# Two chained MLP layers behind a linear-attention stage: block 0's up projections as 256-token half-products

## The chip, the core and the metric

One core of one Trainium2 chip runs the whole program. The metric is device time in microseconds (us), lower is better. The engines are named as the profile names them: PE is TensorE's matrix multiply, PEld its weight load, DVE is VectorE, ACT is ScalarE, and SP only issues DMAs. All engines run side by side and wait for one another through semaphores; each works through its own instructions in the order in which the program gives them.

## What is computed

```python
gamma = 1.0 - 2.0 ** (-5.0 - np.arange(H))            # B, H, S, D = 2, 8, 768, 64
for t in range(S):
    state = gamma * state + einsum('bhd,bhe->bhde', k[:, :, t], v[:, :, t])
    y[:, :, t] = scale * einsum('bhd,bhde->bhe', q[:, :, t], state)
x = y.transpose(0, 2, 1, 3).reshape(1536, 512)
h = x @ w_in                # 512 -> 2048
x = (h * clip(h + 3, 0, 6) / 6) @ w_out               # layer 0
h = x @ moe2_w_in
out = (h * tanh(log1p(exp(h)))) @ moe2_w_out          # layer 1 (Mish)
```

Matrices are float32. The kernel computes each product of float32 matrices from halves: a high half (the value rounded to the matmul's format, `fp32r`) and a low half (what the rounding left), as high·high + low·high + high·low, so three matmuls stand for one.

## The kernel before, in words

**Tiles.** The 1536 tokens are three blocks of 512 (block 0, 1, 2). For each layer the 2048 hidden features are 16 tiles of 128 (index f), two tiles make a pair p, and two pairs make one of four groups g. An up projection of a tile and a block is 4 slices of the 512 inputs x 3 matmuls = 12 matmuls with 128 rows, 128 weight columns and 512 moving columns. It lands in one PSUM bank (`wk`, four of them), ACT and DVE turn it into g (layer 0: ACT `t` = relu(h + 3), DVE g = min(t, 6)·h; layer 1: ACT Mish). Then ACT writes the high half `gh`, DVE the low half `gl`, and a down projection of 12 matmuls adds the tile to four PSUM banks `acc`. There are 96 of these downs (2 layers x 4 groups x 3 blocks x 4 tiles), and so 96 instructions that write `gl`.

**Pairs of blocks.** Group 0 of layer 0 is *plain*: each block has its own 12-matmul up projections. In the seven other groups, blocks 1 and 2 and the two tiles of a pair are a 2 x 2 block product made with seven products in place of eight (`up_pair`, Winograd's form): products 1, 5, 2, 6, 3, 7, 4 of 6 matmuls each go into three banks X, Y, Z, ACT copies partial sums out (`snap`), DVE adds them (`plus`). Product 6 adds to X once product 1 has been copied, 7 adds to X once 6 has been copied, 4 adds to X once the sum of 7 has been taken. They need sums of weight quarters (`wsh`, `wsl`) and differences of x quarters (`make_forms`: T1 to T4, float32 in buffers `q`). Block 0 stays plain in all eight groups.

**Weights.** They come in as 64-bit words (`raw`) and are converted to float32 with integer operations: per chunk of 512 columns one `abs` (ACT in layer 0, DVE in layer 1) and four DVE operations (L405 to L410 of the listing), then the high half on ACT and the low half on DVE (`halves`). A pair has four chunks: two for up, two for down.

**Order.** `Plan` is a list scheduler that runs when the program is built. Each task has an engine, an assumed duration, buffers and dependencies; `order` fills the engines in order of start time and rank. The ranks of PE's work come from a loop that walks `downs` and `ups` with a clock: a down goes as soon as its source is older than `LEAD`, else the next up product goes; `GATE` holds back layer 1's ups. The attention stage's order is the string `EARLY`, that of its loads `LOADS`.

Of the kernel before, what the change touches and what calls it, by code (L numbers as in the profile page):

```python
# [35 lines left out]
BUFS = dict(wk=4, raw=2, cvu=1, cvd=2, t=1, gh=2, gl=2, E=2, R=2,  # L36
            qk=3, kv=3, A=2, kp=1, qs=1, st=3, qtab=2, rawA=1, wbh=3, wbl=3, wsh=3, wsl=3, wdh=4, wdl=4, q=5)

DMA512 = 1.28
MMR = 0.2266  # L40
DVE1 = 0.686
# [5 lines left out]
LEAD = (7.8, 7.5)  # L47
GATE = {'c': 5.0, 'w': 11.5}
EARLY = "sssbkbbkksskkbkbssbhskkbsbkkbohsbohhhhhsosbobohhohoohhoooo"
LOADS = "qk0 mask qk1 qk2 qk3 kv1 kv0 kv2 t1 kv3"  # L50
# [131 lines left out]
def body(ctx: ExitStack, tc: tile.TileContext, aps: dict, out: bass.AP):  # L182
# [37 lines left out]
    def wk():  # L220
        return buf("wk", [P, 512], "wk")
# [103 lines left out]
    def sq_up(u):  # L325
        seq(u, (12 if u[0] == "c" else 6) * MMR)
# [19 lines left out]
    while i < ND or hq < len(ups):  # L346
        nxt = ups[hq] if hq < len(ups) else None
        gate = 0.0
        if nxt and nxt[1] == 1:
            gate = max((done_at.get(b, 1e9) + GATE[nxt[0]]) for b in ((nxt[3],) if nxt[0] == "c" else (1, 2)))  # L350
# [23 lines left out]
    wbase, wsum, wdown = {}, {}, {}  # L374
    ld_w = [None]
    n_raw = [0]

    def words_of(layer, f, half, cb, col):

        nm = f"w{layer}_{f}_{half}"  # L380
        n_raw[0] += 1
        early = layer == 0 and f < 2 * NP and n_raw[0] % 3 == 0
        rb = buf("att", [P, 512], "rawA", I64) if early else buf("fix", [P, 512], "raw", I64)
        src = aps["w1" if layer == 0 else "w2"][f, half]
        ld = add(nm, "SP", DMA512, [], [rb], lambda: nc.sync.dma_start(out=rb.tile, in_=src))
        ld.after = ld_w[0]
        ld_w[0] = ld

        def words():
            w = rb.tile.bitcast(I32).rearrange("p (n t) -> p n t", t=2)  # L390
            return w[:, :, 0], w[:, :, 1]

        def c():
            return cb.tile[:, col:col + 512]

        def ci():
            return cb.tile.bitcast(I32)[:, col:col + 512]
        if layer == 0:
            a0 = add(nm + "abs", "ACT", act(512), [ld], [rb, cb],
                     lambda: A.activation(c(), words()[1].bitcast(F32), AF.Abs))  # L400
        else:
            a0 = add(nm + "abs", "DVE", dve(512, False), [ld], [rb, cb],
                     lambda: V.tensor_scalar(ci(), words()[1], 0x7FFFFFFF, None, ALU.bitwise_and))
        a1 = add(nm + "c", "DVE", dve(512, False), [a0], [cb],
                 lambda: V.tensor_scalar(c(), c(), TOP_MAX, TOP_MIN, ALU.min, ALU.max))  # L405
        a2 = add(nm + "t", "DVE", dve(512, False), [a1], [cb],
                 lambda: V.tensor_scalar(ci(), ci(), 3, 0x3FFFFFF8, ALU.logical_shift_left, ALU.bitwise_and))
        a3 = add(nm + "o1", "DVE", dve(512), [a2], [cb, rb], lambda: V.scalar_tensor_tensor(
            out=ci(), in0=words()[0], scalar=29, in1=ci(), op0=ALU.logical_shift_right, op1=ALU.bitwise_or))
        a4 = add(nm + "o2", "DVE", dve(512), [a3], [cb, rb], lambda: V.scalar_tensor_tensor(  # L410
            out=ci(), in0=words()[1], scalar=-0x40000000, in1=ci(), op0=ALU.bitwise_and, op1=ALU.bitwise_or))
        if early:
            att_tasks.append(a4)
        return a4

    def halves(nm, cb, c0, n, hb, lb, h0, deps):

        a = add(nm + "hi", "ACT", act(n), deps, [cb, hb],
                lambda: A.copy(hb.tile[:, h0:h0 + n], cb.tile[:, c0:c0 + n]))
        return a, add(nm + "lo", "DVE", dve(n), [a], [cb, hb, lb], lambda: V.tensor_tensor(  # L420
            out=lb.tile[:, h0:h0 + n], in0=cb.tile[:, c0:c0 + n], in1=f32(hb.tile)[:, h0:h0 + n],
# [4 lines left out]
    def make_pair(layer, p):  # L426
        nm = f"u{layer}_{p}"
        cb = buf("fix", [P, 1024], "cvu")
        bh, bl = buf("fix", [P, 1024], "wbh", F32R), buf("fix", [P, 1024], "wbl", F32R)
        sums = not plain[layer, p // NP]  # L430
        early = layer == 0 and p == 0

        def down(k):
            f = 2 * p + k
            db = buf("fix", [P, 512], "cvd")
# [437 lines left out]
```

## Time and profile before

| | us |
|---|---|
| median of 3 runs | 564.93 (564.76 to 565.51) |
| the profiled execution | 564.76 |
| its span, first to last instruction | 563.0 |
| PE busy | 549.9 (98%) |
| DVE busy | 416.1 (74%) |
| ACT busy | 275.5 (49%) |

The profiled execution's own time is 1.8 us more than its span. Busy time is the time in which at least one instruction of the engine was running. Matmul records overlap, since the end of one lies behind the start of the next, so the time that one matmul costs is read from start to start.

### The profile page before, as it was taken

The numbers are of one execution on the slowest core, as the hardware profiler recorded it, in microseconds if no ns is written. First come the engines' busy times: TensorE is split into PE (matmuls) and PEld (weight loads), VectorE is DVE, ScalarE is ACT, GpSimd is POOL, SyncE is SP. The second block draws the span as 40 slices with busy tenths as digits, with TensorE's granted clock in tenths as the row PEclk, the third lists the DMA queues.
The fourth block names the chain that finished last, engine by engine and source line by source line (L and its number), as shares of the span: only waits on it lengthen the run. The fifth ranks groups of instructions, "written<-read, shape, count | busy, mean of one in ns | idle before, by whom it ended". The sixth has DMA issues, their size and how long they took to land.

```text
span 563.0 us, 7604 instructions
## 1 busy us (share of the span) xinstructions
PE 549.9 (98%) x2932; PEld 455.9 (81%) x2932; DVE 416.1 (74%) x730; ACT 275.5 (49%) x506; POOL 0.2 (0%) x4
## 2 busy tenths in 40 slices
PE   6899999999999999999999999999999999999997
PEld 5798888887888888887888888888888888888875
DVE  2899998589959983689999999699426997821433
ACT  3899553665526533454537644534524442423330
POOL 0000000000000000000000000000000000000000
PEclk9999999999999999999999999999999999999999
DMA  8995323022312330013121124224200233000103
GB/s 334 399 358 205 113 76 119 33 75 76 101 49 75 115 111 1 1 38 113 37 76 34 42 75 116 72 79 150 72 0 2 77 111 112 1 0 2 75 17 133
DMA packets 15301, 51.66 MB, mean 92 GB/s; under 512 B 1697, under 2 KB 1697, under 8 KB 15265
## 3 DMA queue, kind: packets, MB, share of 16 engines
q1 hardware_dynamic: 15264, 51.17, 27.2%
q8 instruction: 23, 0.38, 0.3%
q14 instruction: 14, 0.11, 0.1%
HBM read 48.02 MB, written 3.15 MB: 91 GB/s over the span
## 4 chain that ended last, share of the span: by engine, by line
PE 90%; DMA 3%; DVE 3%; ACT 3%; SPq 0%; issue 0%; DVEq 0%; ACTq 0%
PE acc L214 49%; PE wk L214 41%; DMA qk<-in_qk_dram 2%; DMA kv<-in_kv_dram 2%; ACT kp L503 1%; DVE sb L768 0%; DVE g L685 0%; SPq L228 0%; DVE gs L622 0%; DVE wdl L420 0%; ACT st L524 0%; ACT q L569 0%; DVE gs L685 0%; ACT t L621 0%; DVE wsl L420 0%
## 5 line engine op out<-in xcount | busy, mean ns | idle before, releaser
L717 DVE TENSOR_TENSOR gl<-g,gh 128x512 fp32r<-128x512 f32 x68 | 46.8, 689 | 39.5 <-ACT gh L715 32.3
L214 PE MATMUL acc<-gh,wdh 128*128 128x512 f32 x192 | 75.0, 391 | 0.4 <-ACT gh L715 0.4
L214 PE MATMUL acc<-gl,wdh 128*128 128x512 f32 x192 | 74.8, 390 | 0.2 <-DVE gl L717 0.2
L214 PE MATMUL acc<-gh,wdl 128*128 128x512 f32 x192 | 74.7, 389 | 0.0
L214 PE MATMUL acc<-wdh,gh 128*128 128x512 f32 x192 | 74.7, 389 | 0.0
L214 PE MATMUL acc<-wdl,gh 128*128 128x512 f32 x192 | 74.7, 389 | 0.0
L214 PE MATMUL acc<-wdh,gl 128*128 128x512 f32 x192 | 74.7, 389 | 0.0
L715 ACT CAST gh<-g 128x512 fp32r<-128x512 f32 x68 | 42.3, 622 | 40.9 <-PE acc L214 28.6
L214 PE MATMUL wk<-xch,wbh 128*128 128x512 f32 x128 | 50.0, 391 | 0.0
L214 PE MATMUL wk<-xcl,wbh 128*128 128x512 f32 x128 | 49.8, 389 | 0.0
L214 PE MATMUL wk<-xch,wbl 128*128 128x512 f32 x128 | 49.8, 389 | 0.0
L214 PEld LDWEIGHTS acc<-gh,wdh 128*128 128x128 f32 x192 | 36.0, 188 | 8.7 <-ACT gh L715 0.8
L214 PEld LDWEIGHTS acc<-gl,wdh 128*128 128x128 f32 x192 | 36.0, 188 | 8.1 <-DVE gl L717 0.6
L214 PEld LDWEIGHTS acc<-wdh,gh 128*128 128x128 f32 x192 | 36.0, 188 | 7.5
L214 PEld LDWEIGHTS acc<-wdl,gh 128*128 128x128 f32 x192 | 36.0, 188 | 7.5
L214 PEld LDWEIGHTS acc<-wdh,gl 128*128 128x128 f32 x192 | 36.0, 188 | 7.5
L214 PEld LDWEIGHTS acc<-gh,wdl 128*128 128x128 f32 x192 | 36.0, 188 | 7.4
L715 ACT CAST gh<-gs 128x512 fp32r<-128x512 f32 x28 | 17.5, 624 | 33.8 <-PE acc L214 33.6
L685 DVE TENSOR_TENSOR g<-wk,g 128x512 f32<-128x512 f32 x22 | 15.2, 690 | 24.6 <-PE wk L214 23.2
L717 DVE TENSOR_TENSOR gl<-gs,gh 128x512 fp32r<-128x512 f32 x28 | 19.3, 688 | 18.5 <-ACT gh L715 13.6
L214 PE MATMUL wk<-q,wsh 128*128 128x512 f32 x84 | 32.7, 389 | 0.0
L621 ACT ACTIVATE t<-wk,bias 128x512 f32<-128x512 f32 x30 | 20.6, 688 | 21.9 <-PE wk L214 17.8
(116 smaller groups left out, 1110.0 us busy)
## 6 DMA issues: line engine op xcount, KB each, us to landing
raw<-in_w_dram SPq DMA_DIRECT2D x62, 512.0 KB, 3.5
kv<-in_kv_dram SPq DMA_DIRECT2D x12, 516.0 KB, 7.0
qk<-in_qk_dram SPq DMA_DIRECT2D x12, 512.0 KB, 6.9
out_dram<-sb SPq DMA_DIRECT2D x12, 256.0 KB, 2.1
qtab<-in_tabs_dram SPq DMA_DIRECT2D x5, 256.0 KB, 7.2
rawA<-in_w_dram SPq DMA_DIRECT2D x2, 512.0 KB, 7.4
mask<-in_mask_dram SPq DMA_DIRECT2D x1, 512.0 KB, 4.3
```

What stands on the lines that cost most here:

```text
L214: nc.tensor.matmul(o, l, r, start=start, stop=stop, skip_group_check=True)
L503: A.activation(kpb.tile[:, hs], kb.tile[:, hs], AF.Copy, scale=kb.tile[:, 2 * DM + h:2 * DM + h + 1])
L621: lambda: A.activation(tb.tile, src.tile, AF.Relu, bias=bias3))
L685: return add(f"c{k}_{nm}", "DVE", DVE1, deps, [ps, gb], lambda: V.tensor_tensor(out=gb.tile, in0=ps.tile, in1=gb.tile, op=ALU.add))
L715: a = add(f"hi{i}", "ACT", act(512), [tg, prev_split[0]], [gb, gh], lambda: A.copy(gh.tile, gb.tile))
L717: lambda: V.tensor_tensor(out=gl.tile, in0=gb.tile, in1=f32(gh.tile), op=ALU.subtract))
```

## The change

- **Block 0 as a pair.** In the seven groups that are not plain, block 0's tokens are cut into halves of 256, and the halves and the two tiles of a pair go through the same seven products (`up_pair` with `who` = "v"), each of 6 matmuls with 256 moving columns. Both halves share a bank: X and Y use columns 0 to 255, Z columns 256 to 511. Per pair two plain up projections (24 matmuls of 512 columns) become 42 matmuls of 256 columns.
- **New work for that.** Per pair three ACT copies and three DVE sums of 256 columns; g of the second tile in two halves; block 0's x in float32 (buffers `qc`) and its four differences with their halves, once per layer.
- **PSUM.** `wk` (four banks) becomes two rings of two, `wx` for X and `wy` for Z and Y; plain products and scores alternate between them.
- **Weights.** 1024 columns are converted at a time (the first pair of layer 0 still 512). A quarter of the up weights that only the plain product reads is now kept for plain pairs alone, in `tv`, so that `wbh` and `wbl` shrink to 768 columns.
- **Order.** Product 4 stands behind the first product of the next pair; `EARLY`, `LOADS`, `LEAD`, `GATE` have new values.

```diff
+GG, GS = 4, 4
-            qk=3, kv=3, A=2, kp=1, qs=1, st=3, qtab=2, rawA=1, wbh=3, wbl=3, wsh=3, wsl=3, wdh=4, wdl=4, q=5)
+            qk=3, kv=3, A=2, kp=1, qs=1, st=3, qtab=2, wbh=3, wbl=3, wsh=3, wsl=3, wdh=4, wdl=4, q=5, qc=5, tv=2)
-LEAD = (7.8, 7.5)
-GATE = {'c': 5.0, 'w': 11.5}
+LEAD = (7.2, 6.1)
+GATE = {'c': 8.0, 'w': 8.5, 'v': 8.0}
...
-            if k == "p":
+            if k == "p" or kind != "plain":
                 for p in range(g * NP, (g + 1) * NP):
-                    ups.extend(("w", layer, p, n) for n in (1, 5, 2, 6, 3, 7, 4))
+                    ups.extend(("w" if k == "p" else "v", layer, p, n) for n in (1, 5, 2, 6, 3, 7, 4))
...
+    for n in range(len(ups) - 2, -1, -1):
+        if ups[n][0] != "c" and ups[n][3] == 4 and ups[n + 1][0] == ups[n][0] and ups[n + 1][1] == ups[n][1]:
+            ups[n], ups[n + 1] = ups[n + 1], ups[n]
...
+    def words_of(layer, p, half, cb, parts):
+        rb = buf("fix", [P, 1024], "raw", I64)
...
+            n = 1024 // parts
...
+            a1 = add(nm + "c", "DVE", dve(n, False), [a0], [cb],
...
-    def make_forms(layer, after):
+    def make_forms(layer, who):
...
+            ba, bb, n = 0, 0, TB // 2
+            ta, tb = slice(0, TB // 2), slice(TB // 2, TB)
...
-    def up_pair(layer, p):
-        X, Y, Z = wk(), wk(), wk()
+    def up_pair(who, layer, p):
+        X, Z, Y = wk("x"), wk("y"), wk("y")
+        nm = f"{who}{layer}_{p}"
+        forms = tform[layer, who]
+        if who == "w":
+            pass_us, first, last = MMR, slice(0, TB), slice(0, TB)
...
+            pass_us, first, last = MMH, slice(0, TB // 2), slice(TB // 2, TB)
+            g11, g21 = [gbuf(layer, 2 * p + k, 0) for k in range(2)]
+            g12, g22 = g11, g21
...
+            gval[layer, f, 0] = (g11, [mish_or_swish(f"{layer}_{f}_0", layer, g11, [c11, c12])])
+            gval[layer, f + 1, 0] = (g22, [mish_or_swish(f"{layer}_{f + 1}_0d", layer, g22, [c22], last),
+                                           mish_or_swish(f"{layer}_{f + 1}_0c", layer, g22, [p4], first, X)])
```

On PE, at the turn from the second to the third group of layer 0, block 0's up projections of the third group stand before as four plain products (`wk`; `xch`, `xcl` are block 0's halves, `wbh`, `wbl` those of the weights), with a down behind:

```order
L214 MATMUL wk_1797<-xch_169,wbh_1343 128x512
L214 MATMUL wk_1797<-xch_169,wbl_1354 128x512
L214 MATMUL wk_1797<-xcl_192,wbh_1343 128x512
...
L214 MATMUL wk_1823<-xch_169,wbh_1343 128x512
...
L214 MATMUL wk_1849<-xch_169,wbh_1493 128x512
...
L214 MATMUL wk_1875<-xch_169,wbh_1493 128x512
...
L214 MATMUL acc_486_1756<-gh_1845,wdh_1414 128x512
```

At the same turn after, products of three pairs follow each other (the first matmul of each; `wx_1551`, `wx_1612`, `wx_1815` are the pairs' X, `tv` and `qc` hold differences of block 0's x): 4 of the first pair, then 5, 6, 2, 3 and 7 of the second around it, 1 of the third, 4 of the second.

```order
L216 MATMUL wx_1551<-tv_1209,wbh_1014 128x256
...
L216 MATMUL wy_1767<-xch_162,wsh_1376 128x256
...
L216 MATMUL wx_1612<-tv_1286,wsh_1376 128x256
...
L216 MATMUL wy_1789<-xch_162,wbh_1317 128x256
...
L216 MATMUL wx_1612<-xcl_183,wsh_1376 128x256
...
L216 MATMUL wx_1815<-xch_162,wbh_1480 128x256
...
L216 MATMUL wx_1612<-tv_1209,wbh_1317 128x256
```

Between product 7 of the second pair and its product 4 there is one product of another pair; the plain products waited for no copy.

On DVE, at the turn from layer 0 to layer 1, the work before (`cvd` a weight chunk, `gs` a pair's sum, `xcl` block 0's new x, `gl` a down's low half):

```order
L405 TENSOR_SCALAR cvd_3003<-cvd_3003 128x512
L458 TENSOR_TENSOR cvu_2747<-cvu_2747 128x256
L407 TENSOR_SCALAR cvd_3003<-cvd_3003 128x512
L784 TENSOR_TENSOR xcl_3021<-sb_382_1046,xch_2971 128x512
L408 SCALAR_TENSOR_TENSOR cvd_3003<-raw_2780,cvd_3003 128x512
L685 TENSOR_TENSOR gs_659_2930<-wk_2884,gs_659_2930 128x512
L420 TENSOR_TENSOR wsl_3036<-cvu_2747,wsh_3019 128x1024
L410 SCALAR_TENSOR_TENSOR cvd_3003<-raw_2780,cvd_3003 128x512
```

and after, with the chunk at 1024 columns, block 0's x in halves, and its differences behind (`qc`):

```order
L419 TENSOR_SCALAR cvd_3106<-cvd_3106 128x1024
L781 TENSOR_TENSOR gl_3122<-g_638_3104,gh_3112 128x512
L421 TENSOR_SCALAR cvd_3106<-cvd_3106 128x1024
L855 TENSOR_TENSOR xcl_3098<-qc_3068,xch_3033 128x256
L422 SCALAR_TENSOR_TENSOR cvd_3106<-raw_2775,cvd_3106 128x1024
L855 TENSOR_TENSOR xcl_3098<-qc_3070,xch_3033 128x256
L424 SCALAR_TENSOR_TENSOR cvd_3106<-raw_2775,cvd_3106 128x1024
...
L623 TENSOR_TENSOR qc_3027<-qc_3035,qc_3027 128x512
...
L623 TENSOR_TENSOR qc_3035<-qc_3070,qc_3035 128x512
```

Fewer and longer conversions, with a down's low half and block 0's x in the gaps between them, and new differences of x in the same stretch.

## Rows read from the trace of the kernel before

**Rows 1.** The page: busy time and share of PE and DVE, granted clock in 40 slices.
```profile
PE 549.9 (98%) x2932; PEld 455.9 (81%) x2932; DVE 416.1 (74%) x730; ACT 275.5 (49%) x506; POOL 0.2 (0%) x4
...
PEclk9999999999999999999999999999999999999999
```

**Rows 2.** The page: chain that ended last, by engine.
```profile
PE 90%; DMA 3%; DVE 3%; ACT 3%; SPq 0%; issue 0%; DVEq 0%; ACTq 0%
```

**Rows 3.** Busy time by stretch (us from the span's start; columns named in the first line).
```profile
core 0: us, PE busy (x) PEld busy (x) DVE busy (x) ACT busy (x) POOL busy (x), PEclk, DMA share, GB/s
0.00:32.00 32.00, 25.28 (x376) 22.05 (x376) 18.91 (x34) 20.96 (x66) 0.20 (x4) 1.00 0.95 366
...
245.00:353.00 108.00, 107.10 (x473) 88.31 (x472) 103.14 (x184) 56.63 (x90) 0.00 (x0) 1.00 0.24 71
353.00:388.00 35.00, 35.00 (x156) 28.96 (x156) 27.84 (x53) 16.47 (x27) 0.00 (x0) 1.00 0.29 89
...
540.00:563.00 23.00, 18.40 (x80) 14.56 (x79) 9.87 (x15) 5.50 (x9) 0.00 (x0) 0.97 0.25 92
```

**Rows 4.** Waits of PE: total us, times, longest.
```profile
PE wk L214 <- DMA qk<-in_qk_dram: 2.6, 2, 1.5
...
PE wk L214 <- ACT gs L682: 0.9, 1, 0.9
PE wk L214 <- DVE g L685: 0.9, 1, 0.9
```

**Rows 5.** Matmuls of block 0's plain products, one of three such rows.
```profile
L214 PE MATMUL wk<-xch,wbh 128*128 128x512 f32 x128 | 50.0, 391 | 0.0
```

**Rows 6.** Timeline (start us, length us): a run of 512-column matmuls and one load.
```profile
149.64 0.39 PE L214 MATMUL wk<-xch,wbl 128*128 128x512 f32 x1
...
150.10 0.39 PE L214 MATMUL wk<-xch,wbh 128*128 128x512 f32 x1
150.10 0.19 PEld L214 LDWEIGHTS wk<-xch,wbl 128*128 128x128 f32 x1
...
155.99 0.39 PE L214 MATMUL acc<-gl,wdh 128*128 128x512 f32 x1
```

**Rows 7.** Timeline: the first loads and matmuls after a wait of PE.
```profile
259.95 0.19 PEld L214 LDWEIGHTS wk<-xbl,wsh 128*128 128x128 f32 x1 [1.32 <-ACT gs L682]
259.96 0.50 PE L214 MATMUL wk<-xbl,wsh 128*128 128x512 f32 x1 [0.90 <-ACT gs L682]
260.06 0.19 PEld L214 LDWEIGHTS wk<-xbl,wsl 128*128 128x128 f32 x1
260.30 0.40 PE L214 MATMUL wk<-xbl,wsl 128*128 128x512 f32 x1
```

**Rows 8.** Timeline of DVE where it runs without a gap.
```profile
313.53 0.68 DVE L768 SCALAR_TENSOR_TENSOR sb<-acc,sb 128x512 f32<-128x512 f32 x1
314.13 0.42 DVE L458 TENSOR_TENSOR cvu<-cvu 128x256 f32<-128x256 f32 x1
314.46 0.68 DVE L420 TENSOR_TENSOR wdl<-cvd,wdh 128x512 fp32r<-128x512 f32 x1
...
315.40 0.42 DVE L403 TENSOR_SCALAR cvd<-raw 128x512 int32<-128x512 int32 x1
315.73 0.42 DVE L458 TENSOR_TENSOR cvu<-cvu 128x256 f32<-128x256 f32 x1
...
318.88 1.22 DVE L420 TENSOR_TENSOR wsl<-cvu,wsh 128x1024 fp32r<-128x1024 f32 x1
320.01 0.68 DVE L410 SCALAR_TENSOR_TENSOR cvd<-raw,cvd 128x512 int32<-128x512 int32 x1
```

**Rows 9.** Timeline of DVE: the 36th and the 64th of the 96 `gl`.
```profile
244.67 0.69 DVE L717 TENSOR_TENSOR gl<-gs,gh 128x512 fp32r<-128x512 f32 x1
...
388.35 0.69 DVE L717 TENSOR_TENSOR gl<-g,gh 128x512 fp32r<-128x512 f32 x1
```

**Rows 10.** Groups by shape: ACT copies of 256 and of 512 columns out of PSUM.
```profile
L569 ACT COPY q<-acc 128x256 f32<-128x256 f32 x16 | 5.4, 381 | 1.5 <-DVE xal L563 1.5
...
L682 ACT COPY g<-wk 128x512 f32<-128x512 f32 x22 | 12.9, 587 | 18.3 <-PE wk L214 18.3
```

More of the change, by code (lines that the diff above doesn't have):

```diff
@@ L372, in body @@
     t_warm = add("warm", "PE", 1.8, [z0], [zb] + kv_acc, run_warm, -99)
-    wbase, wsum, wdown = {}, {}, {}
+    wbase, wquart, wsum, wdown = {}, {}, {}, {}
     ld_w = [None]
[L376 to L414, printed above, removed]
@@ L427, in make_pair @@
         nm = f"u{layer}_{p}"
[L428 to L431, printed above, removed]
-        def down(k):
-            f = 2 * p + k
-            db = buf("fix", [P, 512], "cvd")
-            dh, dl = buf("fix", [P, 512], "wdh", F32R), buf("fix", [P, 512], "wdl", F32R)
-            t = words_of(layer, f, 1, db, 0)
-            hi, lo = halves(f"d{layer}_{f}", db, 0, 512, dh, dl, 0, [t, gate_hi[0]])
-            gate_hi[0] = hi
-            wdown[layer, f] = (dh, dl, lo)
@@ L441, in make_pair @@
-        base = []
-        for k in range(2):
-            t = words_of(layer, 2 * p + k, 0, cb, 512 * k)
-            hi, lo = halves(nm + f"b{k}", cb, 512 * k, 512, bh, bl, 512 * k, [t, gate_hi[0]])
-            gate_hi[0] = hi
-            base.append(lo)
-            wbase[layer, 2 * p + k] = (bh, bl, lo)
-            if early:
+        parts = 2 if layer == 0 and p == 0 else 1
+        cb, db = buf("fix", [P, 1024], "cvu"), buf("fix", [P, 1024], "cvd")
+        bh, bl = buf("fix", [P, 768], "wbh", F32R), buf("fix", [P, 768], "wbl", F32R)
@@ new lines, in make_pair, with base @@
+        av = buf("fix", [P, 512], "tv", F32R) if plain[layer, p // NP] else None
+        up_words, down_words = words_of(layer, p, 0, cb, parts), words_of(layer, p, 1, db, parts)
+        n = 1024 // parts
+        def base(k):
+            t = up_words(k)
+            m = n if parts == 1 else 512 - 256 * k
+            lo = [halves(nm + f"b{k}", cb, n * k, min(m, 768), bh, n * k, bl, n * k, [t])]
+            if av and (k or parts == 1):
+                lo.append(halves(nm + "v", cb, 768, 256, av, 0, av, 256, [t]))
+            for j in range(2 // parts):
+                wbase[layer, 2 * p + k + j] = (bh, bl, lo)
+            wquart[layer, p] = av
+            return lo
@@ L449, in make_pair @@
+        def down(k):
+            t = down_words(k)
+            for j in range(2 // parts):
+                f = 2 * p + k + j
+                dh, dl = buf("fix", [P, 512], "wdh", F32R), buf("fix", [P, 512], "wdl", F32R)
+                wdown[layer, f] = (dh, dl, halves(f"d{layer}_{f}", db, 512 * (k + j), 512, dh, 0, dl, 0, [t]))
+        prev = []
+        for k in range(parts):
+            prev.extend(base(k))
+            if parts > 1:
                 down(k)
-        if sums:
+        if not plain[layer, p // NP]:
@@ new lines, in snap, with plus @@
+        def snap(k, ps, pc, gb, gc, dep):
+            return add(f"s{k}_{nm}", "ACT", act(n), [dep] + (att_tasks if gb.tag[:2] == "gs" else []), [ps, gb],
+                       lambda: A.copy(gb.tile[:, gc], ps.tile[:, pc]))
+        def plus(k, ps, pc, gb, gc, deps):
+            return add(f"c{k}_{nm}", "DVE", dve(n), deps, [ps, gb], lambda: V.tensor_tensor(
+                out=gb.tile[:, gc], in0=ps.tile[:, pc], in1=gb.tile[:, gc], op=ALU.add))
+        p1 = product(1, X, True, first, [])
```

334 lines of the change are left out of this document (195 added, 139 removed).

## The prediction

> **What bounds the kernel now.** I read the page's busy times first, then the chain that ended last, the stretches, PE's waits, and last the timeline for the pace of single instructions. PE is busy for 98% of the span [rows 1], and 90% of the chain that ended last is PE [rows 2]. The reader is to see that nothing else sets the end: PE's waits in the MLP part add up to about 2 us, each of the two longest 0.9 us, behind a copy and a sum of a pair [rows 4]. Two stretches are exceptions: the first 32 us, in which PE works for 25.3 while the DMA engines are 95% busy, and the last 4 us behind the last matmul [rows 3]. The granted clock stands at full, the 2.4 GHz level, in every slice [rows 1]. So a matmul fewer is time gained, as long as DVE and ACT keep up. DVE is the one to watch. Its 74% [rows 1] is a mean: from 245 to 353 us, the turn from layer 0 to layer 1, where conversions need their `abs` on DVE too, it is busy for 103.1 of 108.0 us, and PE still for 107.1 [rows 3]. There two engines are full at once.
>
> **PE's work.** Block 0's plain products outside group 0 are 7 groups x 4 tiles x 12 = 336 matmuls of 512 columns: 112 of the 128 in the row and in its two sisters [rows 5]. One costs 0.2268 us: from 149.64 to 155.99 lie 28 starts [rows 6]. That is 76.2 us, all of it on the path. In their place stand 14 pairs x 42 = 588 matmuls of 256 columns, which no row shows in this format. The lower bound is half of 0.2268, 0.1134 us. The other bound keeps what a 512-column matmul takes above its columns: at one column per cycle of the 2.4 GHz level (my assumption; it fits) 512 are 0.2133 us, so 0.0135 is on top, and 0.1067 + 0.0135 = 0.1202. Can the load of 128 weight columns be hidden under so short a stream? A load is recorded with 0.19 us [rows 6], but after a wait the second load starts 0.11 us behind the first, while the first is still on record [rows 7]: a load holds its place for 0.11 us, and in the steady run it starts with the matmul ahead of it [rows 6]. 0.11 lies just inside 0.1134 to 0.1202, so the load is hidden, by almost nothing. I take the middle, 0.1168, since nothing tells whether the 0.0135 scales: 588 x 0.1168 = 68.7 us, a gain of **7.5 us** (9.5 to 5.5).
>
> **DVE's work.** The conversions of two chunks become one. At DVE's pace without gaps a two-input operation of 256, 512 and 1024 columns takes 0.33, 0.60 and 1.13 us, and a one-input one of 512 columns 0.33 [rows 8]. One of 1024 isn't shown; 0.60 is my estimate, by the same ratio as from 256 to 512. Merging two operations saves only about 0.07 us. Against that stand 42 sums of 256 columns, eight differences and eight low halves of 512 for block 0, and smaller pieces. Where it counts, I added up DVE's program between the 36th and the 64th `gl`, which the trace has at 244.67 and 388.35 us [rows 9]: before, 24 x 0.33 + 137 x 0.60 + 62 x 0.33 + 14 x 1.13 = 127 us (237 instructions) in 143.7 us, a share of 88%. After: 60 x 0.33, 81 x 0.60, 6 of 768 columns at 0.87 (estimated between), 32 one-input ones of 1024 at 0.60 and 36 x 1.13 make 134 us (215 instructions). PE's work between the same downs falls from 648 x 0.2268 = 147.0 to 492 x 0.2268 + 252 x 0.1168 = 141.0 us. So DVE's work grows by 7 where PE's shrinks by 6, and DVE would have to work at 95% through the whole stretch. In its tightest part it now reaches 95.5% by busy time, with PE hardly waiting [rows 3]; over the whole stretch it has needed 88%. I take 93.5%, nearer to the tight part because that shows what DVE does when it is wanted: 134/0.935 = 143.4, so **2.5 us** of PE's gain are lost there (0 at 95%; 10 at 88%, which is the rival below).
>
> **Chains in a pair.** Product 7 must wait until ACT has copied the result of 6, and 4 until DVE has added 7's. At 512 columns such a copy takes 0.587, at 256 columns 0.381 us [rows 10]. A product of another pair in between is now 6 x 0.117 = 0.70 us and no longer 1.36. A result can be used once the last matmul is through: 0.39 from start to end for 512 columns [rows 6], so some 0.28 for 256. 0.28 + 0.38 is 0.66 against 0.12 + 0.70 = 0.82 us, so one product hides the copy if ACT is free, and ACT has half of its time free [rows 1]. With DVE, in the order shown above, it is 0.28 + 0.42 = 0.70; but what is queued ahead there may now be a conversion of 1.22 us that cannot be broken off. A whole such wait costs up to 1 us, as the two longest did [rows 4]. Most products have two or more products or a down between; about five places have one. I add **0.5 us** (0 to 2). Behind product 4, the second half of g and the down wait too, but with several us in hand.
>
> **Edits at nothing.** The loads carry the same bytes in the same queue; `kv0` ahead of the mask, and 1 MB pieces, move arrivals in the first 32 us, where PE waits 2.6 us for `qk` [rows 4]: 0, between -1 and +1. The eight more ACT copies in the attention stage lie in an engine that works for 21 of the first 32 us [rows 3]. The order of the last two pairs of layer 1 still ends with 6, 3, 7, 4, so the wait of 0.9 us for `g` at the end stays [rows 4]. The rings of two banks cost nothing that I can find: X, which lives longest, no longer stands in the way of Y and Z.
>
> **The sum.** The profiled execution took 564.8 us with a span of 563.0, and the median of the runs is 564.9, so the two can be read as one. 564.8 - 7.5 + 2.5 + 0.5 = **560.3 us**.
>
> **Rivals.** (a) *The excess does not scale and DVE keeps up.* At 0.1134 us a matmul and no loss in the stretch: 564.8 - 9.5 = 555.3. For it: the tight stretch hides its full load now. Against it: nothing there has slack on either engine. The Trainium skill, "TensorE: Matmul & The Clock Gate", section "Back-to-back issue gap", goes further and gives a gap of N/2.4 + 2.5 ns, which is 109 ns at 256 columns; by it the matmuls would take 64.2 us and the total would be near 556 with the losses above. The row differs already at 512: 0.2268 [rows 6] against 0.2158.
>
> (b) *DVE becomes the bound.* If in the stretch it gets no more than the 88% that it has now, because it goes on waiting in order for banks and copies, the stretch takes 134/0.883 = 151.8 us, 10.8 over PE's work: 564.8 - 7.5 + 0.5 + 10.8 = 568.6, slower than before. The turn from gain to loss is a share of 90.5%, where the stretch loses 7 us. For it: 7 us more work on an engine that is full for 108 us; longer instructions in front of urgent ones. Against it: of the 17 us that DVE does not use in the stretch now, only 5 lie in the tight part [rows 3]; the others lie where PE was the one to be waited for.
>
> (c) *The load is not hidden.* If it stood ahead of every stream, a matmul would cost 0.11 + 0.113 = 0.223, 588 of them 131 us: 564.8 - 76.2 + 131 + 0.5 = 620. Against it: every load of the steady run starts with the matmul ahead [rows 6]. The same page of the Trainium skill, section "The mechanism" of Part 3, says that a load overlaps running matmuls only when its row group differs. Here all rows are used by every matmul and the loads overlap all the same, at 512 columns; no run shows 256.
>
> (d) *The gain is eaten but not more*, a share near 91%: 563 to 566.5, no measurable change.
>
> **How the numbers follow.** A difference under 0.2%, 1.1 us, can't be told from none. Forecast, 557.5 to 563: 0.50. Rival (a) and between, down to 554.5: 0.17; below that 0.04. Rival (d): 0.13, of which 0.02 counts as faster and 0.11 as the same. Rival (b), 566.5 and above: 0.13. Rival (c): 0.03. Faster 0.73, same 0.11, slower 0.16. The range 554.5 to 566.5 holds the first two and (d), 0.80. Its low end is the cheaper matmul with DVE keeping up and the start 1 us early; its high end 0.1202 a matmul with 5 us lost in the stretch, 2 in the chains and 1 at the start (567), less a little.
>
> **What would show it.** In the profile after: 256-column matmuls that start 0.113 to 0.120 us apart; if 0.13 or more, the first term is wrong and nothing is gained. DVE busy for over 95% around the turn of the layers, and PE's waits there on `gl`, `xcl` or a sum, 2 to 3 us in total; 0 is rival (a), 8 and more rival (b). Waits of X's product 4 on DVE or 7 on ACT that add up to under 2 us. The attention stage ending within 1 us of before. What would make it wrong most easily is DVE.

## The result and the profile after

The changed kernel takes **556.19 us** (median of 4 runs, 556.02 to 557.15) against 564.85 us in the same comparison (564.68 to 565.51): a ratio of 0.985, 95% interval 0.983 to 0.987. It is faster by 8.7 us, where 4.5 were forecast; the range of 554.5 to 566.5 holds it. The profiled execution took 556.31 us with a span of 554.5.

The page of the changed kernel, PE's busy time, the granted clock in 40 slices and the chain by engine, stands against [rows 1, 2]:

```profile
PE 544.5 (98%) x3184; PEld 463.7 (84%) x3184; DVE 421.3 (76%) x651; ACT 289.7 (52%) x553; POOL 0.2 (0%) x4
...
PEclk9999999999999999999999999999999999999999
...
PE 95%; DMA 3%; DVE 1%; SPq 0%; issue 0%
```

252 more matmuls are done in 5.4 us less busy time, and the chain that ended last is now 95% PE and no longer 90%: waits have gone from it. The first two stretches of [rows 3], and under them PE's waits as in [rows 4]:

```profile
0.00:32.00 32.00, 26.65 (x348) 22.77 (x349) 20.29 (x37) 23.04 (x73) 0.20 (x4) 1.00 0.96 376
245.00:353.00 108.00, 107.98 (x541) 91.63 (x540) 104.31 (x164) 62.19 (x108) 0.00 (x0) 1.00 0.20 69
```

```profile
PE wy L216 <- DMA qk<-in_qk_dram: 3.4, 4, 1.6
PE acc L216 <- DVE t L377: 1.5, 1, 1.5
PE wx L216 <- DVE g L745: 0.8, 1, 0.8
PE acc L216 <- DVE qs L529: 0.4, 1, 0.4
```

DVE is busy for 104.3 of 108 us around the turn of the layers, 1.2 more than before, and PE for 107.98: it waits there for next to nobody (two steps at 325 us are 0.3 us too long). Of the MLP's waits one is left, the one at the end.

Where the 8.45 us between the two profiled executions lie, added up from the starts of all matmuls:

| | before | after | gain, us |
|---|---|---|---|
| block 0's products outside group 0 | 336 x 0.2267 = 76.2 | 588 steps, 70.3 without waits | 5.9 |
| first down behind the attention stage starts at | 60.92 | 59.27 | 1.65 |
| steps over 20 ns too long behind 66 us (waits), sum of the excess | 3.55 | 1.82 | 1.7 |
| 512-column steps of 229 to 247 ns in the place of 226.7, excess | 0.13 (23) | 0.74 (118) | -0.6 |
| behind the start of the last matmul | 4.1 | 4.3 | -0.2 |

The sum is 8.45. 102 of the 118 steps in the fourth line are among the first five 512-column matmuls behind a run of halves. The row of the second line, of the kernel before and then of the changed one:

```profile
60.92 0.50 PE L214 MATMUL acc<-gh,wdh 128*128 128x512 f32 x1
```

```profile
59.27 0.50 PE L216 MATMUL acc<-gh,wdh 128*128 128x512 f32 x1
```

### The profile page after: what moved, and what is told of

The parts are those of the page before. It is cut to its first block, busy times and chain, and to the rows that moved or that the text cites. A ratio compares the mean times of both kernels' runs of the same rounds, so it can differ in the third digit from the quotient of the medians.

```text
span 554.5 us, 8001 instructions
## 1 busy us (share of the span) xinstructions
PE 544.5 (98%) x3184; PEld 463.7 (84%) x3184; DVE 421.3 (76%) x651; ACT 289.7 (52%) x553; POOL 0.2 (0%) x4
## 3 DMA queue, kind: packets, MB, share of 16 engines
q1 hardware_dynamic: 10944, 51.17, 25.8%
## 4 chain that ended last, share of the span: by engine, by line
PE 95%; DMA 3%; DVE 1%; SPq 0%; issue 0%
PE acc L216 51%; PE wx L216 24%; PE wy L216 20%; DMA qk<-in_qk_dram 3%; DVE sb L834 0%; SPq L235 0%; DVE g L745 0%
## 5 line engine op out<-in xcount | busy, mean ns | idle before, releaser
L779 ACT CAST gh<-g 128x512 fp32r<-128x512 f32 x68 | 42.2, 621 | 30.3 <-PE acc L216 18.2
L745 DVE TENSOR_TENSOR g<-wy,g 128x256 f32<-128x256 f32 (+1 forms) x42 | 21.4, 509 | 28.6 <-PE wy L216 28.4
L781 DVE TENSOR_TENSOR gl<-gs,gh 128x512 fp32r<-128x512 f32 x28 | 19.3, 688 | 22.7 <-ACT gh L779 16.9
L431 ACT CAST wdh<-cvd 128x512 fp32r<-128x512 f32 x32 | 19.7, 620 | 20.6 <-PE acc L216 16.3
L433 DVE TENSOR_TENSOR wdl<-cvd,wdh 128x512 fp32r<-128x512 f32 x32 | 21.9, 686 | 10.9 <-ACT wdh L431 10.5
L742 ACT COPY g<-wx 128x256 f32<-128x256 f32 (+1 forms) x42 | 18.5, 441 | 21.2 <-PE wx L216 20.9
L834 DVE SCALAR_TENSOR_TENSOR sb<-acc,sb 128x512 f32<-128x512 f32 x36 | 23.3, 685 | 4.5 <-PE acc L216 4.5
L431 ACT CAST wsh<-cvu 128x1024 fp32r<-128x1024 f32 x14 | 14.7, 1051 | 21.1 <-DVE cvu L477 21.0
```

The lines of the kernel that those rows point to most:

```text
L433: return add(nm + "lo", "DVE", dve(n), [a], list(dict.fromkeys([cb, hb, lb])), lambda: V.tensor_tensor(out=lb.tile[:, l0:l0 + n], in0=cb.t ...
L742: lambda: A.copy(gb.tile[:, gc], ps.tile[:, pc]))
L745: return add(f"c{k}_{nm}", "DVE", dve(n), deps, [ps, gb], lambda: V.tensor_tensor(out=gb.tile[:, gc], in0=ps.tile[:, pc], in1=gb.tile[:, g ...
L779: a = add(f"hi{i}", "ACT", act(512), tg + [prev_split[0]], [gb, gh], lambda: A.copy(gh.tile, gb.tile))
L781: lambda: V.tensor_tensor(out=gl.tile, in0=gb.tile, in1=f32(gh.tile), op=ALU.subtract))
L834: lambda d=d, ac=ac: V.scalar_tensor_tensor(out=sb.tile[:, d, :], in0=ac.tile, scalar=sc, in1=sb.tile[:, d, :], op0=ALU.mult, op1=ALU.add) ...
```

## The experiments

The plan sets a new order for every edit, so a run's time holds the edit and the order that follows from it. The table splits each profiled run's distance from the changed kernel's 556.31 us in the same way as above. "Start" is the end of the attention stage, with 0.2267 us taken off for each 512-column matmul that stands ahead of it beyond the changed kernel's 39; "late" is the excess of late steps behind 66 us; "products" is the 5.9 us of block 0's products less the 0.5 us by which 512-column steps beside halves are longer. The runs are numbered by their labels. Ratios are against the kernel before, on the same chip; on the chips of these runs it took 564.6 to 565.2 us. Each split rests on one profiled execution, and e9's (568.4 us) is among the slowest of its 12, 2.3 us above their median.

| run | median us | ratio, 95% | profiled - 556.31 | products | start | late |
|---|---|---|---|---|---|---|
| changed kernel | 556.2 | 0.983 to 0.987 | | | | (1.8) |
| e1 block 0 plain, one ring | 571.4 | 1.010 to 1.013 | 15.4 | 5.4 | -0.2 | 10.2 |
| e2 chunks of 512 | 564.2 | 0.998 to 1.000 | 7.9 | 0 | 0.2 | 7.8 |
| e3 loads and first steps of before | 560.7 | 0.992 to 0.995 | 3.7 | 0 | 3.5 | 0.2 |
| e5 halves alone (one ring) | 582.9 | 1.031 to 1.034 | 25.8 | 0 | 2.6 | 22.7 |
| e6 conversions alone | 576.1 | 1.018 to 1.023 | 21.0 | 5.4 | 4.1 | 11.6 |
| e7 one ring | 573.5 | 1.014 to 1.017 | 17.8 | 0 | -0.4 | 17.9 |
| e8 DVE + 4.8 us | 558.9 | 0.987 to 0.991 | 3.2 | 0 | 0.9 | 2.1 |
| e9 halves and rings | 566.0 | 0.999 to 1.003 | 12.1 | 0 | 4.5 | 8.0 |
| e10 lead of before | 559.0 | 0.988 to 0.991 | 2.8 | 0 | -0.1 | 3.0 |
| e11 DVE + 9.6 us | 562.1 | 0.993 to 0.996 | 5.5 | 0 | 0 | 5.3 |
| e12 last down moved | 555.4 | 0.981 to 0.985 | -0.1 | 0 | 1.0 | -1.1 |

**e4, the price of a matmul.** A kernel of series of 48 matmuls and nothing else:

```
for s, n in enumerate((512, 256, 384, 256, 320, 224, 192, 128)):
    for i in range(48):        # each with the next of four 128-column weight tiles
        nc.tensor.matmul(t[:, 0:n], w[:, c:c + 128], x[:, 0:n], ...)
```

> A measurement of TensorE's price alone; nothing of the reference's computation is in it. Series of 48 matmuls in the kernel's format (fp32r, 128 rows, each with its own load of 128 weight columns) of 512, 256, 384, 256, 320, 224, 192 and 128 columns, then 512 and 256 in turn. Theory (a fixed excess of 13.4 ns on top of one column per cycle at the 2.4 GHz level): 227, 120, 173, 120, 147, 107, 93 and 67 ns from start to start, and 347 for a pair of 512 and 256. Rival 1 (a share of 1/16 on top): 227, 113, 170, 113, 142, 99, 85, 57. Rival 2 (what a 256-column matmul takes is the load's own 0.11 to 0.12 us): 320 and 384 columns with less than 13 ns on top, and 0.11 to 0.12 us for 256, 224, 192 and 128 alike.

Mean time from start to start, at a granted clock of 1.00:

| columns | 512 | 384 | 320 | 256 | 224 | 192 | 128 |
|---|---|---|---|---|---|---|---|
| ns | 226.7 | 173.5 | 146.7 | 119.8 | 111.5 | 111.5 | 111.0 |
| above columns / 2.4 | 13.4 | 13.5 | 13.4 | 13.1 | 18.2 | 31.5 | 57.7 |

The theory holds from 512 down to 256: 13.1 to 13.5 ns on top whatever the length. Below that it fails, and rival 2 has the floor: 0.111 us for 224, 192 and 128 columns alike, 8 ns under the price of 256. So at 256 columns it is the fixed excess that is paid, and the load of the weights is still hidden. In turn, a 512 takes 235.8 and a 256 behind it 117.2 ns (without the series' first step): 6.5 ns more for the pair than alone. In the changed kernel the first five 512s behind a run of halves take 233, 236, 228, 233 and 231 ns, some 27 ns in all; that both have one cause is not shown. The Trainium skill, "TensorE: Matmul & The Clock Gate", section "Back-to-back issue gap", puts 2.5 ns on top of N/2.4 for the gap of a matmul taken by itself; in this kernel's format, with a load for each matmul, e4 shows 13 ns or more at every length.

**e1, block 0 plain.** Block 0 keeps its plain products, the other parts stay, save the banks:

```diff
-BUFS = dict(wx=2, wy=2, raw=2, ...)
+BUFS = dict(wk=4, raw=2, ...)
...
-            if k == "p" or kind != "plain":
+            if k == "p":
...
-        if b == 0 or plain[layer, g]:
+        if plain[layer, g]:
```

> The changed kernel with block 0 as before: 336 plain matmuls of 512 columns outside group 0 in the place of 588 of 256. The conversions of 1024 columns, the order of the loads and the shorter lead stay; the banks are one ring of four, since the plan finds no order for plain block 0 in two rings of two. Theory (the half-products are the gain, and each 256-column matmul keeps the whole excess of a 512-column one): 588 x 0.1204 = 70.8 us against 336 x 0.2267 = 76.2, so 5.4 us slower than the changed kernel, about 561.6 us, of 560.5 to 563, and its DVE has less to do. Rival 1 (the gain lies in the conversions, the loads and the lead): within 1 us of the changed kernel, 555.5 to 557. Rival 2 (all of the 8.7 us hang on the products): 564 to 565.

It took 571.4 us, beyond every case named. Its products cost the expected 5.4 us by their steps, but PE also waits 10.2 us more, so its time alone says nothing on the price of halves. Either the waits belong to plain block 0 or to the ring; e7 has halves and the same waits.

**e7, one ring of four banks**, with everything else of the change:

```diff
-BUFS = dict(wx=2, wy=2, raw=2, ...)
+BUFS = dict(wk=4, raw=2, ...)
...
-        return buf("wk", [P, 512], "w" + kind)
+        return buf("wk", [P, 512], "wk")
```

> The changed kernel with one ring of four banks in the place of two rings of two. Theory (the rings cost and give nothing by themselves): 555.5 to 557.5. Rival (X, which lives longest, stands in the way of Y and Z in a common ring): PE waits for a bank or behind ACT and DVE at the places where products follow each other, 558 to 562.

573.5 us: the theory that the rings give nothing falls, and the rival is right in kind and too small by far. The change loses all of its gain and 9 us more without the two rings. PE's waits in e7:

```profile
PE acc L216 <- ACT gh L779: 4.8, 3, 2.8
PE wk L216 <- DVE g L745: 4.1, 5, 1.0
...
PE acc L216 <- DVE gl L781: 1.6, 3, 0.9
...
PE wk L216 <- DVE gs L745: 0.8, 1, 0.8
```

Lines 2 and 4 are product 4 right behind product 7. First such a place in e7, the last matmul of 7 and the first of 4; then the same place of the program in the changed kernel (the third product 4 of a pair of blocks 1 and 2, behind as many downs), where another pair's product 5 stands between (`wx<-xbl,wsh` begins 7, `wy<-xbh,wsh` begins 5, `t4h`,`wbh` is 4):

```profile
213.57 0.39 PE L216 MATMUL wk<-q,wsh 128*128 128x512 f32 x1
214.75 0.50 PE L216 MATMUL wk<-t4h,wbh 128*128 128x512 f32 x1 [0.78 <-DVE g L745]
```

```profile
206.91 0.39 PE L216 MATMUL wx<-xbl,wsh 128*128 128x512 f32 x1
...
208.27 0.39 PE L216 MATMUL wy<-xbh,wsh 128*128 128x512 f32 x1
...
209.40 0.39 PE L216 MATMUL wy<-q,wsh 128*128 128x512 f32 x1
209.63 0.39 PE L216 MATMUL wx<-t4h,wbh 128*128 128x512 f32 x1
```

The next pair's first products need banks while X is still held. With X in a ring of its own they have them; in a common ring the plan put nothing there, and PE stands for 0.9 to 1.2 us. (That it is X's bank which is missing is argued from the program, not tested by itself.) There are six such places in e7, 5.8 us, and one in the changed kernel. The waits for `gh` and `gl` between 129 and 146 us make another 6.4, low clock included, and many shorter waits the rest of the 19.7 us of late steps. The waits for `gh` show a further price, that of the clock: one of 2.8 us that ends at 143.5 us is followed by 2.5 us at a granted clock of 0.50, the 1.2 GHz level, in which PE is busy all the time (columns as in [rows 3]):

```profile
140.50:143.50 3.00, 0.17 (x1) 0.00 (x0) 2.40 (x4) 2.41 (x4) 0.00 (x0) 0.94 0.95 303
143.50:146.00 2.50, 2.50 (x6) 1.89 (x7) 2.50 (x5) 1.05 (x2) 0.00 (x0) 0.50 0.13 56
146.00:149.00 3.00, 3.00 (x22) 2.76 (x21) 2.96 (x4) 0.67 (x3) 0.00 (x0) 0.91 0.00 0
```

Six matmuls in 2.5 us, some 1.5 us of loss behind that wait. Why the waits for `gh` come at this place in all four kernels with one ring that keep other parts of the change (e1, e5, e6, e7), and hardly in the kernel before, which has one ring too, was not settled. All four also keep product 4 behind the next pair's first product, an edit that no run undoes by itself; so the ring's price is that of one ring together with this order.

**e5 and e9, half-products alone.** e5 takes the half-products and leaves the loads, the order of the first steps, the lead, the chunks and the ring as before; e9 is the same with the two rings. e9's diff (e5 has that of e7 besides):

```diff
-LEAD = (7.2, 6.1)
+LEAD = (7.8, 7.5)
...
-EARLY = "ssbsksbkskkbkksbbhkskbsbbksbokhoshbhshhoosbohobohbohoohhhooo"
-LOADS = "qk0 kv0 mask qk1 qk2 kv1 kv2 t1 kv3 qk3"
+EARLY = "sssbkbbkksskkbkbssbhskkbsbkkbohsbohhhhhsosbobohhohoohhoooo"
+LOADS = "qk0 mask qk1 qk2 qk3 kv1 kv0 kv2 t1 kv3"
...
-        parts = 2 if layer == 0 and p == 0 else 1
+        parts = 2
```

> Block 0's half-products and little else: the changed kernel with weights converted 512 columns at a time, one ring of four banks, and the loads, the order of the first steps and the lead of the kernel before. Theory A (the 5.4 us of cheaper products are a gain of their own): 559.3 us, 558 to 560.5. Theory B (as the second run of this study, with chunks of 512, showed: half-products add DVE work in the stretch around the turn of the layers, PE waits there 3 us in one place and 1.3 in another, and the granted clock then falls to 0.5 for some 6 us, which costs about 3 more): 5.4 us of gain and 6 to 10 of new waits, 563 to 569, with a wait of PE for DVE between 300 and 350 us that is the longest of the program.

> Block 0's half-products with the two rings of banks, and nothing else of the change: conversions of 512 columns, the loads, the order of the first steps and the lead are those of the kernel before. It differs from the fifth run of this study (582.9 us) by the rings alone. Theory A (each part has its price whatever the others are: 8.0 us for the conversions and 4.5 us for the start, measured singly on the changed kernel): 556.2 + 8.0 + 4.5 = 568.7 us, 566 to 571, slower than the kernel before. Theory B (with the rings the half-products give their 5.4 us, and the 8.0 of the conversions was the accident of one order): 558.5 to 562. In both, the rings are worth more than 10 us beside the fifth run, since product 4 no longer stands right behind product 7; if they were worth less than 5, the ring's price of 17 us would have been an accident too.

e5 took 582.9 us, above both theories; its longest wait is not in the stretch that theory B named, but its waits are everywhere (22.7 us of late steps). e9 took 566.0 us: theory A, at its lower edge. Between e5 and e9 lies only the ring, and 16.9 us, against 17.3 between e7 and the changed kernel. So the price of the common ring is no accident of one order. e9's longest wait is 3.5 us at 333 us, for a sum that DVE does late, as in e2 below with the same chunks of 512. In its first 17 us the granted clock is 0.50 for 6.8 us, so its 4.5 us of start are not the loads' order alone. And half-products with rings, but without the conversions and the loads, are no faster than the kernel before.

**e6, conversions alone**: e1 with the loads, first steps, lead and gates of before.

```diff
-LEAD = (7.2, 6.1)
-GATE = {'c': 8.0, 'w': 8.5, 'v': 8.0}
+LEAD = (7.8, 7.5)
+GATE = {'c': 5.0, 'w': 11.5}
```

> The conversions of 1024 columns without half-products: block 0 plain, one ring of four banks, and the loads, the order of the first steps, the lead and the gates of the kernel before. Theory (the conversions by themselves take work from DVE where PE does not wait for it, so they give nothing, and one buffer for a down's words in the place of two may cost a wait): 564 to 566.5. Rival (chunks of 1024 are what makes the changed kernel faster): 556 to 561. If plain block 0 with these conversions needs its waits whatever the lead, as the first run of this study had them at 130 and 141 us: 569 to 572.

576.1 us: slower than every case. 10.3 of its 13.4 us of late steps lie where e1 has its waits for `gh`, here from 134 and 147 us on. That conversions of 1024 columns are the whole gain is refuted. What they cost by themselves is not shown, since e6 also keeps product 4's new place, the smaller buffers and block 0's x in float32.

**e2, conversions of 512 columns** in the changed kernel.

```diff
-        parts = 2 if layer == 0 and p == 0 else 1
+        parts = 2
```

> The changed kernel with every layer's weights converted 512 columns at a time, as before, where the changed kernel takes 1024. Theory (DVE has next to nothing left in the stretch between the 36th and the 64th gl, where it needed 143.0 us for work that I added up to 134): some 48 conversions of 1024 become 96 of 512, at about 0.07 us more for each pair of instructions, 28 chunks x 2 halves x 4 to 5 instructions around the stretch, about 3 to 4 us more work for DVE there, of which at most 1 to 2 us reach the end, since the down behind the 64th gl still has 1.2 us in hand: 557 to 559. Rival (the larger chunks save nothing that counts, or shorter instructions stand less in the way of urgent ones): 555 to 556.5.

564.2 us, all of the gain gone. The theory had the place right (DVE in the stretch) and the size wrong: I thought of 1 to 2 us behind the 64th `gl`. The wait comes at 323 us and is one of the longest of the study. PE's two waits:

```profile
PE wy L216 <- DVE gs L746: 3.0, 1, 3.0
PE wy L216 <- ACT gs L743: 1.6, 2, 1.3
```

PE stands because the next product needs the bank of an earlier product 3, which DVE has not yet added into `gs`. The product was through by 302.6 us, and the sum's other operand is a copy by ACT behind the same pair's product 6, first row, that is there from 310.05 us on. The rows below it are what DVE does from 321 us to the sum:

```profile
309.46 0.59 ACT L743 COPY gs<-wx 128x512 f32<-128x512 f32 x1 [0.66 <-PE wx L216]
```

```profile
321.02 0.69 DVE L624 TENSOR_TENSOR qc<-qc,qc 128x512 f32<-128x512 f32 x1
321.62 0.69 DVE L433 TENSOR_TENSOR wdl<-cvd,wdh 128x512 fp32r<-128x512 f32 x1
...
323.16 0.69 DVE L624 TENSOR_TENSOR qc<-qc,qc 128x512 f32<-128x512 f32 x1
323.76 0.42 DVE L421 TENSOR_SCALAR cvd<-cvd 128x512 int32<-128x512 int32 x1
324.10 0.69 DVE L624 TENSOR_TENSOR qc<-qc,qc 128x512 f32<-128x512 f32 x1
324.70 0.69 DVE L629 TENSOR_TENSOR qc<-qc,xch 128x512 fp32r<-128x512 f32 x1
325.30 0.69 DVE L422 SCALAR_TENSOR_TENSOR cvd<-raw,cvd 128x512 int32<-128x512 int32 x1
325.91 0.69 DVE L746 TENSOR_TENSOR gs<-wy,gs 128x512 f32<-128x512 f32 x1
```

DVE has no gap in these rows. The sum that PE needs has its turn 15.9 us after it could run, behind block 0's differences (`qc`), lows of block 0 and steps of conversions that were put ahead of it. In the changed kernel the same sum comes 10.7 us after it could, at 320.42 us, and PE waits for nothing there. Behind the wait the granted clock is 0.50 from 327.6 to 334.4 us:

```profile
327.00:329.00 2.00, 0.70 (x7) 0.50 (x6) 2.00 (x5) 1.94 (x5) 0.00 (x0) 0.65 0.04 8
329.00:331.00 2.00, 2.00 (x5) 1.61 (x6) 1.53 (x3) 1.35 (x3) 0.00 (x0) 0.50 0.87 260
331.00:333.00 2.00, 2.00 (x7) 1.52 (x6) 1.05 (x3) 0.32 (x1) 0.00 (x0) 0.50 0.63 256
333.00:335.00 2.00, 2.00 (x7) 1.62 (x6) 1.58 (x4) 0.80 (x2) 0.00 (x0) 0.64 0.00 0
```

Eleven whole steps of 427 ns in the place of 227 are 2.2 us, and 2.7 with the broken ones beside them.

**e3, loads and first steps of before** in the changed kernel (the `EARLY` and `LOADS` lines of e9's diff).

> The changed kernel with the order of the first 32 us as before: the order of the loads (mask ahead of kv0 and qk2) and the order in which the first weight conversions and block 0's steps are started. Theory (the attention stage's last 512-column matmul stands 1.65 us earlier in the changed kernel with as much work ahead of it, so this order is worth that): 557.8 us, 557.3 to 558.3, with the last 512-column matmul of the attention stage back at about 60.7 us. Rival (the 1.65 us come from block 0's halves and its smaller copies, or are taken back behind it): within 0.5 us of the changed kernel.

560.7 us. The theory is right in kind, at twice its size: in the profile the start costs 3.5 us, not 1.65, and nothing is taken back behind; the median is 4.5 us above the changed kernel's. PE's waits that the changed kernel has not, all in the first 66 us:

```profile
PE acc L216 <- DVE A L533: 1.5, 1, 1.5
PE acc L216 <- DVE xbl L583: 0.9, 1, 0.9
...
PE acc L216 <- ACT qc L589: 0.7, 1, 0.7
```

One is the attention's own `A`, the other two are steps for the halves and forms of the blocks (`xbl`, `qc`), at which PE does not stop with the new order.

**e8 and e11, more work for DVE in the stretch**: one clamp more (e8) and two (e11) in each conversion of layer 1's first four pairs.

```diff
+            for r in range(1 if layer == 1 and p < 4 else 0):
+                a1 = add(nm + f"x{r}", "DVE", dve(n, False), [a1], [cb],
+                         lambda: V.tensor_scalar(c(), c(), TOP_MAX, TOP_MIN, ALU.min, ALU.max))
```

> The changed kernel with one more clamp of 1024 columns (which changes no value) in each of the eight conversions of layer 1's first four pairs: 8 x 0.60 = 4.8 us more for DVE, all between the 36th and the 64th gl. Theory (DVE has nothing left there; the lead at the end of the stretch is down to 1.2 us): PE waits 3.5 us or more, and where that falls in one place the granted clock falls behind it and costs some 3 us more: 559.5 to 565. Rival (DVE's full share in the stretch is work that could as well be done later, since the plan moves conversions to where there is room): 556 to 557.5.

> The changed kernel with two more clamps of 1024 columns in each of the eight conversions of layer 1's first four pairs, 9.6 us more for DVE in the stretch between the 36th and the 64th gl. With 4.8 us the kernel took 558.9 us, 2.7 more. Theory (that took what slack there was, and every further us counts in full): 563.7 us, and up to 566 if PE waits over 2.5 us in one place and the granted clock falls behind that. Rival (DVE catches up behind the stretch at the same rate): 561.5.

558.9 and 562.1 us: 2.7 and 5.9 more, by the late steps 2.1 and 5.3. DVE's slack is not zero, and more than half of each added us reaches the end. e8 falls a little short of its theory (3.3 at least), e11 between its two. PE and DVE in 245 to 353 us of e11, and its two waits for DVE there:

```profile
245.00:353.00 108.00, 103.80 (x516) 86.68 (x515) 105.15 (x167) 58.82 (x102) 0.00 (x0) 1.00 0.20 64
```

```profile
PE wy L216 <- DVE gs L748: 2.1, 1, 2.1
PE wx L216 <- DVE gs L748: 1.7, 2, 0.9
```

DVE gains 0.8 us of busy time in this window and PE loses 4.2: there PE now waits for DVE. Behind the wait of 2.1 us the granted clock stays at 1.00.

**e10, lead of before** (the `LEAD` line of e9's diff).

> The changed kernel with the lead of the kernel before: a down's place in PE's order is at least 7.8 us (layer 0) and 7.5 us (layer 1) behind its product in the place of 7.2 and 6.1. Theory (the lead at the end of the stretch was eaten, not missing, so more of it has no wait to take away): 555.7 to 558. Rival 1 (with more lead the two waits at 325 us go): 555.2 to 555.7. Rival 2 (a down that comes later keeps its g and its conversions' room longer, and PE waits for those): 559 to 564.

559.0 us, the lower edge of rival 2. Two of PE's waits are new; the second is for the low half of a weight sum:

```profile
PE wx L216 <- DVE g L745: 1.9, 2, 1.1
...
PE wy L216 <- DVE wsl L433: 1.3, 1, 1.3
```

A longer lead takes nothing away from the waits, and puts others in.

**e12, one down moved** between products 7 and 4 of the last pair.

```diff
+    late = pe_rank[ups[-1]]
+    before6 = max(n for n in range(ND) if pe_rank["o", n, 0] < pe_rank[ups[-4]])
+    for d in range(4):
+        pe_rank["o", before6, d] = late - 0.01 + 0.001 * d
```

> The changed kernel with one down moved: the 12 matmuls of the down ahead of the last pair's products 6, 3 and 7 stand between its products 7 and 4. Theory (PE waits 0.95 us in front of that product 4 for DVE's sum of product 7, the last wait that stayed, and 2.72 us of a down cover it): 555.2 us, 554.9 to 555.6. Rival (the wait only moves, to the copy behind product 6 or to the down behind): 556.0 to 556.8.

All of PE's waits in e12:

```profile
PE wy L216 <- DMA qk<-in_qk_dram: 2.4, 2, 2.0
PE acc L216 <- DVE t L382: 1.5, 1, 1.5
PE acc L216 <- DVE qs L534: 0.4, 1, 0.4
```

The wait for `g` is gone and none has come in its place, as the theory said. The median, 555.4 us (554.63 to 556.22), is 0.75 below the changed kernel's, but their intervals overlap; the profiled run shows why so little can be told. Its first stage is the same program, and it ended 1.0 us later (the first down behind it):

```profile
60.28 0.50 PE L216 MATMUL acc<-gh,wdh 128*128 128x512 f32 x1
```

That down starts at 59.27 in the changed kernel's profile, at 59.25 in e11's and at 60.16 in e8's. So the end of this stage, which waits for the first loads, scatters by about 1 us between executions. In e12's profile a wait of 2.0 us for `qk` ends at 9.7 us, and from 10.1 to 13.5 us the granted clock is 0.50; e8 has no such fall, but its waits for `qk` are longer than the changed kernel's (4.0 against 3.4 us). Of e12's four runs, the two with a mean clock of 0.999 took 554.6 and 554.8 us, the two with 0.995 took 556.1 and 556.2.

## Why the prediction was right, and where it was not

**PE's price: the gain was taken too high.** Both bounds were right and the choice between them wrong. Twelve matmuls of 256 columns in a row start from 168.01 to 169.34 us, 0.121 us apart:

```profile
168.01 0.28 PE L216 MATMUL wx<-xcl,wsh 128*128 128x256 f32 x1
...
169.34 0.28 PE L216 MATMUL wx<-xcl,wbh 128*128 128x256 f32 x1
```

463 of 588 steps are 120 ns, the upper bound, not 0.1168. The term is 5.9 us, or 5.3 with the 512-column steps beside halves, and not 7.5. I took the middle "since nothing tells whether the 0.0135 scales"; e4 tells that it does not. Seven eighths of the columns (588 x 256 for 336 x 512) cost 0.92 of the time, not 0.875. That the load stays hidden was right, by 8 ns; rival (c) had no ground.

**DVE's stretch: length right, consequence wrong.** The 36th and the 64th `gl` of the changed kernel, against [rows 9]:

```profile
240.18 0.69 DVE L781 TENSOR_TENSOR gl<-gs,gh 128x512 fp32r<-128x512 f32 x1 [1.43 <-ACT gh L779]
...
383.23 0.68 DVE L781 TENSOR_TENSOR gl<-g,gh 128x512 fp32r<-128x512 f32 x1
```

The first matmuls that read the 36th and the 64th, in the changed kernel and then in the kernel before:

```profile
242.72 0.39 PE L216 MATMUL acc<-gl,wdh 128*128 128x512 f32 x1
...
385.10 0.39 PE L216 MATMUL acc<-wdh,gl 128*128 128x512 f32 x1
```

```profile
247.11 0.39 PE L214 MATMUL acc<-gl,wdh 128*128 128x512 f32 x1
...
395.20 0.39 PE L214 MATMUL acc<-wdh,gl 128*128 128x512 f32 x1
```

DVE's stretch is 143.05 us (143.4 forecast). But 2.5 us lost to PE were forecast, and PE lost next to nothing: between these two reads it took 142.38 us (148.09 before), for 141.9 us of work at 0.2267 and 0.1204 a matmul. The step that failed takes 93.5% for the most that DVE can do, sets the time between two of DVE's results equal to PE's time between the same places, and books the difference as a wait of PE. DVE did work at 133.5/143.05 = 93.3%, by the count of its instructions in the trace at the prediction's prices (the estimate of 0.60 us for a one-input operation of 1024 columns held: 0.60), but PE did not wait for it. That the length came out is luck, since the share was chosen as a limit and was none. The 0.7 us by which DVE's stretch is longer than PE's came out of the time that a result lies before it is used: 1.85 us behind the 36th `gl`, 1.19 behind the 64th. The gap behind a single `gl` says little (behind the 64th it fell from 6.17 to 1.19 us, behind the 63rd it rose from 0.8 to 3.2); its mean over the stretch fell from 3.2 to 2.1 us, with the lead shortened too.

Rival (b) asked the right question all the same. With more work put on it, DVE did 137.2 us by the same count in 145.3 us (e8) and 140.5 in 147.9 (e11), 94.4% and 95.0%; the plan moved part of the work out of the stretch, so these are 3.7 and 7.0 us more, not 4.8 and 9.6. There PE took 2.3 and 5.5 us longer between the same two reads. So DVE had little more to give, and most of what was added was paid; rival (b)'s fall back to 88% is refuted. (The prediction's "10 at 88%" should read 11, from 134/0.88 - 141.0; its sum does not use it.)

**Chains in a pair: sign wrong.** 0.5 us of loss was added; late steps behind 66 us fell by 1.7 us, and no step inside a half-pair is longer than 0.26 us. The waits that went are one for `gh` at 130 us and a product 7's for the copy behind product 6 at 260 us, some 1.1 us each with the slower steps behind them. The estimate that one product between covers a copy or a sum held. What was underrated is why there is a product between: "The rings of two banks cost nothing that I can find" was true and beside the point. Without them the change is 17 us slower (e7; e9 against e5). An edit was costed at nothing because it took no engine's time, and the loss without it was not asked for.

**Start: outside its bounds.** 0 with -1 to +1 was given, and the profiles show -1.65. As the same start scatters by 1 us, the gain is 0.6 to 1.7, about the bound, if the one profile of the kernel before is typical. What e3 adds: the new order is worth 3.5 us to the changed kernel, where the old one makes PE wait for steps of the forms.

**End.** The wait stayed as forecast, 0.8 us in the list of waits; it is not needed, as e12's trace shows.

**The sum.** -7.5 + 2.5 + 0.5 = -4.5 us was forecast. Measured term by term it is -5.3 (products with their neighbours), 0 (DVE), -1.7 (waits), -1.65 (start) and +0.2 (behind the last matmul), -8.45. The sign and the range were right, the range partly by luck: it holds the time because one error (2.2 us too fast, in the products) stood against three (2.5, 2.2 and 1.65 us too slow, in DVE, the chains and the start). The time lies near rival (a)'s 555.3, but not by rival (a)'s price: DVE kept up as it said, the matmuls did not get cheaper than the upper bound.

## What to carry to other kernels

A shorter matmul keeps the whole fixed part of a long one (13 ns here), so count products and columns apart before splitting a product. Work that is added to a second engine costs nothing as long as its results are there when they are wanted, and a busy share alone says neither that it is free nor what it costs: compare what the first engine took between the same two instructions with its work there, and put more work on the second to see where its room ends. An edit that takes no engine's time, a ring of banks or an order of loads, may be the condition under which the others pay: undo it alone, and split the difference into price, start and late steps before believing a total. A plan that sets a new order for every edit makes each such difference one of two orders as well.

## What the runs showed of the hardware

A wait of PE can cost more than its length. Waits of 2.8 us (e7) and 3.0 us (e2) were followed by a granted clock of 0.50, the 1.2 GHz level, for 3 to 6 us with PE busy, at 427 in the place of 227 ns a matmul: 1.5 to 3 us on top. Waits of 2.5 us (e1) and 2.4 us (e6) were followed by it too. Behind 2.1 us (e11), and behind every wait of the kernels before and after in the MLP part, none over 0.9 us, the clock stayed at 1.00. The length of one wait is not all of it: in e5 the clock fell behind a wait of 1.5 us, with another of 0.5 us less than 3 us ahead of it. Waits of 1.3 us and, 1 us later, 0.35 us were followed by 0.50 in e6 (from 137.3 to 140.7 us) and not in e1 (at 130.8 and 131.9 us). What else counts was not tried.

Matmuls with their own load of 128 weight columns did not come closer than 0.111 us on average, for 224, 192 and 128 columns alike (e4). The Trainium skill, "TensorE: Matmul & The Clock Gate", section "LDWEIGHTS (loading the stationary operand)", gives a load columns / 1.2 ns, 107 ns for 128: e4's floor agrees to 5 ns, and so does the 0.11 us from load to load in [rows 7].
